# Four block grams of a decayed linear attention as two grams of 96 columns

## The chip, the cores and the metric

One core of one Trainium2 chip. The metric is device time of one execution in microseconds (us). Executions of one kernel scatter here: the 182 executions of the kernel before in the rounds of the experiments took 601.9 to 610.6 us, with a standard deviation of 1.4. In the 20 profiles the start (the time before the stretch defined below) takes 178.0 to 182.3 us, and what follows the stretch 108.7 us in each. PE's clock is half for 10 to 31 us of it, but the start is not simply longer where there is more half clock (178.0 us in e5 and 182.1 in f3, with 10.2 us each), so why it varies is not shown. By the states on record, all timed executions were in the fast state but one, of s2. Two sizes are used: the whole time (a median), and **the stretch**, which leaves that noisy start out: from the 161st of batch one's 216 z records to the first product of batch four (before: from 178.7 to 492.9 us of the span). It is worked out from the starts of the records in the trace and holds all the changed work of the six units but the making of the new masks.

## The reference, cut to what matters

```python
def _attn_ref(r, k, v, w, u):              # (4, 8, 768, 48) each, u (8, 48)
    for t in range(S):
        cur = np.einsum('bhd,bhe->bhde', u[None] * kt, vt)
        y[:, :, t] = np.einsum('bhd,bhde->bhe', rt, state + cur)
        state = wt[:, :, :, None] * state + np.einsum('bhd,bhe->bhde', kt, vt)

def _moe_ref(x, w_tok1, w_tok2, w_ch1, w_ch2):       # x (4, 768, 384) = y, heads side by side
    xt = x.transpose(0, 2, 1)
    h = np.maximum(xt @ w_tok1, 0.0) @ w_tok2
    u = x + h.transpose(0, 2, 1)
    return u + np.maximum(u @ w_ch1, 0.0) @ w_ch2
```

All is float32. A token's r meets an earlier token's k through the product of all w between the two.

## The kernel before

The kernel works on 12 units of 256 tokens (three per batch). Inside 64 tokens it builds the weights r·k in blocks that double: at block size b (2, 4, 8, 16, 32) `gram` multiplies k of the left block of each pair with r of the right one, a masked copy on VectorE (DVE) takes the wanted squares out of PSUM, and `join` then multiplies k and r by the decay over their block, so that the next size can use them. Units 6 to 11, called the near units (`i >= NEAR`), get the diagonal in another way, and are the only ones that the change touches. The token and channel products of the mixer (h_ps, z_ps, q_ps) fill TensorE (PE) between these pieces: the work of a unit is woven between the mixer products of the batch before it.

```python
        def gram(l):
            b = 1 << l
            ...
            right = r_.rearrange("p (n two b) -> p n two b", two=2, b=b)[:, :, 1, :]
            g = L["g"] = ps_g.tile([128, 2, 512], f32, name="gram")
            for ca in range(UC * A):
                fours(lambda q, j, rows, cols: pe.matmul(
                    g[cols, q, ts(ca, 32)], k_[rows, ds(ca * 128 + j * T, T)],
                    right[rows, ts(2 * ca + j, 32 // b), :], start=True, stop=True))
        ...
        def join(l, w, new):
            ...
            dve.tensor_mul(halves, halves, by)                       # k and r at once, 1024 elements
            dve.tensor_mul(new[:ROWS], wv[:, :, 0], wv[:, :, 1])
        ...
        def block(l):
            gram(l)
            join(l, products[l], products[l + 1])
            pick(l)                                                  # the masked copy
        ...
        for l in range(1, LEVELS):
            pieces.append((1.2, lambda l=l: block(l)))
...
        return [(1.0, begin[1]), tokens, one(carry, rest[0]), update, one(before, rest[1]), one(within, rest[2]),
                *loads, *rest[3:], row0, row1, place]
```

The last line weaves two units: `tokens` (transposes of k), `carry` (products kv_ps), `update` (states, on DVE), `before` and `within` (y_ps) belong to unit i, the pieces `rest` are unit i+1's blocks. `fours` issues four products at a time, one for each quarter of PE's array. The pool of gram tiles has two PSUM buffers, which the transposes xT_ps of batches two and three share. `apool` has two buffers of each name.

## Time and profile before

| | before |
|---|---|
| whole time, median of 3 | 604.07 us (602.54 to 604.15) |
| profiled execution | 601.6 us, mean granted clock 0.983 |
| PE, DVE, ACT busy in the whole span | 95%, 60%, 29% |
| the stretch | 314.20 us |
| of it, PE between two records without work (gaps over 0.1 us) | 2.99 us |

The lines of busy time by engine, by stretch and by group are shown in the prediction. To these belongs one view more, since it is the one that changes most: all waits of PE from 200 us to the end, before the change. Columns: engine, what was waited with, what released it: sum in us, how often, the longest.

```profile
PE gram L307 <- issue: 1.0, 2, 0.7
PE y_ps L476 <- DVE state L457: 0.6, 1, 0.6
PE gram L430 <- DVE rk L341: 0.5, 1, 0.5
PE xT_ps L546 <- DVE x L536: 0.3, 1, 0.3
```

In 400 us PE waits 2.4 us, and only 1.4 us of that is for DVE. Whatever the change saves on PE is gained, and whatever it makes PE wait is lost.

### The profile page before, as it was taken

The page shows a single profiled execution, that of the slowest core. Times are in us where ns is not written, and L with a number is a line of the kernel's source. Part 1 is how long each engine was busy: PE and PEld are TensorE (multiplying, and loading weights), DVE is VectorE, ACT ScalarE, POOL GpSimd, SP SyncE. Part 2 cuts the span into 40 slices and gives each one's busy share as a digit, 9 for nine tenths or more (in the row PEclk, how much of TensorE's full clock was granted, in tenths as well). Part 3 has the DMA queues.
Part 4 walks back from the last instruction along what each step waited for, and adds up shares of the span by engine and source line. Part 5 has one row for each costly group of instructions (what it writes and reads, how often), then busy time and mean ns, then how long its engine had stood idle before and what let it go on. Part 6 is the DMA issues. An engine that isn't in the chain of part 4 may idle for free.

```text
span 601.6 us, 18874 instructions
## 1 busy us (share of the span) xinstructions
PE 570.0 (95%) x8596; PEld 486.6 (81%) x8596; DVE 361.0 (60%) x599; ACT 177.1 (29%) x428; POOL 7.2 (1%) x32
## 2 busy tenths in 40 slices
PE   3787899899999989999999999999999999999997
PEld 2776658776888886789989896789898986898987
DVE  5789699999675867666457376528446422040404
ACT  6155444422433313241141231231313312302020
POOL 4000000000000000000000000000000000000000
PEclk9997599999999999999999999999999999999999
DMA  8534564620233235141124103001200000000000
GB/s 340 195 83 152 163 199 151 208 70 28 82 110 109 67 82 158 29 133 28 53 57 132 28 28 106 2 2 43 65 2 28 2 27 0 1 20 8 27 2 27
DMA packets 22976, 45.85 MB, mean 76 GB/s; under 512 B 2512, under 2 KB 14928, under 8 KB 22896
## 3 DMA queue, kind: packets, MB, share of 16 engines
q1 hardware_dynamic: 22752, 44.64, 23.3%
q8 instruction: 67, 1.10, 0.8%
q14 instruction: 13, 0.11, 0.1%
q10 hardware_dynamic: 144, 0.00, 0.0%
HBM read 39.91 MB, written 4.72 MB: 74 GB/s over the span
## 4 chain that ended last, share of the span: by engine, by line
PE 79%; DVE 13%; DMA 3%; issue 3%; ACT 2%; SPq 0%; DVEq 0%; ACTq 0%
PE z_ps L554 29%; PE q_ps L588 24%; PE gram L307 7%; PE h_ps L534 4%; PE h_ps L527 4%; DVE rk L341 3%; DMA x<-in_w_ch_dram 2%; PE h_ps L564 2%; PE kv_ps L440 2%; PE y_ps L489 2%; PE y_ps L476 2%; PE gram L430 2%; DVE at L323 2%; PE xT_ps L546 1%; DVE scratch L218 1%
## 5 line engine op out<-in xcount | busy, mean ns | idle before, releaser
L554 PE MATMUL z_ps<-xT,wch 128*128 128x256 f32 x864 | 195.9, 382 | 1.6 <-ACT z L556 1.6
L554 PEld LDWEIGHTS z_ps<-xT,wch 128*128 128x128 f32 x864 | 161.0, 190 | 23.8 <-ACT z L556 2.8
L556 ACT ACTIVATE z<-z_ps 128x256 f32<-128x256 f32 x144 | 55.0, 382 | 171.3 <-PE z_ps L554 158.2
L588 PE MATMUL q_ps<-wch,z 128*128 128x192 f32 x528 | 94.6, 329 | 0.0
L588 PEld LDWEIGHTS q_ps<-wch,z 128*128 128x128 f32 x528 | 86.1, 190 | 1.4
L588 PE MATMUL q_ps<-scratch,z 128*128 128x192 f32 x396 | 70.0, 328 | 0.0
L307 PE MATMUL gram<-rk 48*64 48x32 f32 x3072 | 62.7, 234 | 6.6 <-issue 3.2
L307 PEld LDWEIGHTS gram<-rk 48*64 48x64 f32 x3072 | 58.2, 152 | 12.4 <-issue 6.4
L341 DVE TENSOR_TENSOR rk<-rk,decay 112x1024 f32<-112x1024 f32 x36 | 44.0, 1223 | 35.7 <-PE gram L307 26.1
L588 PEld LDWEIGHTS q_ps<-scratch,z 128*128 128x128 f32 x396 | 64.4, 190 | 0.4
L341 DVE TENSOR_TENSOR rk<-rk,w 112x1024 f32<-112x1024 f32 x36 | 44.0, 1223 | 28.9 <-PE gram L307 23.9
L580 DVE TENSOR_TENSOR z<-z 128x768 f32<-128x768 f32 x11 | 10.5, 957 | 65.6 <-ACT z L556 65.6
L527 PE MATMUL h_ps<-x,wtok 128*128 128x384 f32 x96 | 35.6, 518 | 0.0
L534 PE MATMUL h_ps<-h,wtok 128*128 128x384 f32 x96 | 35.3, 492 | 0.0
L323 DVE COPY_PREDICATED at<-mask,gram 128x512 f32<-128x512 uint8 x36 | 32.2, 895 | 0.0
L457 DVE TENSOR_TENSOR state<-state,kv_ps 128x192 f32<-128x192 f32 x40 | 14.2, 356 | 24.4 <-PE kv_ps L440 23.5
L331 ACT COPY at<-gram 16x256 f32<-16x256 f32 x48 | 17.4, 363 | 33.7 <-PE gram L307 32.5
L536 DVE TENSOR_TENSOR x<-x,h_ps 128x384 f32<-128x384 f32 x24 | 13.3, 553 | 23.1 <-PE h_ps L534 23.1
L527 PEld LDWEIGHTS h_ps<-x,wtok 128*128 128x128 f32 x96 | 18.5, 201 | 10.4 <-issue 0.6
L534 PEld LDWEIGHTS h_ps<-h,wtok 128*128 128x128 f32 x96 | 16.4, 190 | 9.6 <-ACT h L529 2.6
L431 ACT COPY kT<-gram 128x512 f32<-128x512 f32 x24 | 14.0, 585 | 28.5 <-PE gram L430 28.3
L318 ACT COPY at<-gram 32x256 f32<-32x256 f32 x48 | 17.4, 363 | 14.2 <-PE gram L301 13.7
(84 smaller groups left out, 514.9 us busy)
## 6 DMA issues: line engine op xcount, KB each, us to landing
rk<-in_rkw_dram SPq DMA_DIRECT2D x36, 192.0 KB, 3.4
x<-in_w_ch_dram SPq DMA_DIRECT2D x10, 512.0 KB, 4.3
vt<-in_v_dram SPq DMA_DIRECT2D x12, 384.0 KB, 4.4
out_dram<-o SPq DMA_DIRECT2D x24, 192.0 KB, 1.9
rp<-in_near_dram SPq DMA_DIRECT2D x12, 384.0 KB, 3.6
scratch<-in_w_ch_dram SPq DMA_DIRECT2D x8, 512.0 KB, 4.3
w<-in_rkw_dram SPq DMA_DIRECT2D x18, 192.0 KB, 3.2
rk<-in_rkw_dram SPq DMA_DIRECT2D x6, 512.0 KB, 6.5
```

What stands on the lines that cost most here:

```text
L307: fours(lambda q, j, rows, cols: pe.matmul(g[cols, q, ts(ca, 32)], k_[rows, ds(ca * 128 + j * T, T)], right[rows, ts(2 * ca + j, 32 // b), ...
L318: act.copy(at[p:p + b, :, ts(c, A), b:], g[ds(p + c * b, b)])
L323: dve.copy_predicated(out=dst, data=g.rearrange("p q (m b) -> p q m b", b=b), mask=masks[l].rearrange("p x t -> p (x t)").rearrange("p (m ...
L331: act.copy(at[p:p + b, :, :, n * 2 * b + b:(n + 1) * 2 * b], g[p:p + b, :, :, ts(n, b)])
L341: dve.tensor_mul(halves, halves, by)
L431: act.copy(L["kT"][:, c], ps)
L457: dve.tensor_add(new, new, got)
L527: pe.matmul(sums[i], wtok1[:, c, ts(i, 128)], xs[bt][:, c, :], start=(c == 0), stop=(c == C - 1))
L534: pe.matmul(ps, wtok2[:, i, ts(c, 128)], h1[:, i, :], start=(i == 0), stop=(i == DTOK // 128 - 1))
L554: pe.matmul(ps, wch1[:, m, ts(jt, 128)], xT[:, m, ts(s, SEG)], start=(m == 0), stop=(m == DM // 128 - 1))
L556: act.activation(zs[s][:, jt, :], ps, AF.Relu)
L588: pe.matmul(ps, a[:, j, :], b[:, j, :], start=(j == 0), stop=(j == HJ - 1))
```

## The change

Block sizes 2 and 4, and sizes 8 and 16, get one gram each. Of four neighbouring blocks (0 to 3) of size b, the pairs of both sizes are (0→1), (0,1→2,3) and (2→3). The moving side holds six groups of columns: r of blocks 1, 2, 3 as they are, and r of blocks 2 and 3 decayed over the one or two blocks between. So 96 columns take the place of two times 32, four grams become two, and k and r are joined over four blocks at once.

```diff
+        def two_blocks(l):
+            b = 1 << l
+            ...
+                t = apool.tile([128, COLS], f32, name="rp")
+                ...
+                act.copy(y[:, :, 0:4:3], of[:, :, 1:3])
+                act.copy(y[:, :, 5], of[:, :, 3])
+                dve.tensor_mul(y[:, :, 1:5:3], of[:, :, 2:4], by[:, :, 1:3]...)
+                dve.tensor_mul(y[:, :, 2], y[:, :, 4], by[:, :, 1]...)
+            for c in range(UC):
+                g = ps_g.tile([128, 2, 512], f32, name="gram")
+                ...
+                    fours(lambda q, j, rows, cols: pe.matmul(
+                        g[cols, q, ts(a, 96)], k_[rows, ds((c * A + a) * 128 + j * T, T)],
+                        rw[c][rows, ts(2 * a + j, 96)], start=True, stop=True))
+            ... (two small products of w, then k by w of three blocks, r from the moving side, new decay)
+            for c in range(UC):
+                ...
+                for q, first in enumerate((0, 3, 5)):
+                    n = (3 - q) * b
+                    dve.copy_predicated(out=to[:, :, :, (q + 1) * b:], data=got[:, :, :, first * b:first * b + n], ...)
 ...
+        if i >= NEAR:
+            return pieces + [(1.8, lambda l=l: two_blocks(l)) for l in (1, 3)] + [(0.9, lambda: block(5))]
         for l in range(1, LEVELS):
             pieces.append((1.2, lambda l=l: block(l)))
 ...  (masks for four blocks, made once; the near rows' loads come one step later, for they share the tiles "rp")
+        if i + 1 >= NEAR:
+            rest[2] = (rest[2][0], lambda f=rest[2][1]: (load_near(i + 1), f()))
```

More of the change, by code (lines that the diff above doesn't have):

```diff
@@ L259, in begin @@
             if i >= NEAR:
+                products[3], products[5] = w_[:, :COLS // 8], decay[:, :COLS // 32]
                 join(0, products[0], products[1])
@@ L353, in block @@
             pick(l)
+        def two_blocks(l):
+            b = 1 << l
+            w = products[l].rearrange("p (g q) -> p g q", q=4)[:ROWS]
+            k = k_.rearrange("p (g q b) -> p g q b", q=4, b=b)[:ROWS]
+            r = r_.rearrange("p (g q b) -> p g q b", q=4, b=b)[:ROWS]
+            G = COLS // (4 * b) // UC
+            rw, gs = [], []
+            for c in range(UC):
+                t = apool.tile([128, COLS], f32, name="rp")
+                rw.append(t)
+                y = t[:, :COLS // UC * 3 // 2].rearrange("p (g s b) -> p g s b", s=6, b=b)[:ROWS]
+                of, by = r[:, ts(c, G)], w[:, ts(c, G)]
+                act.copy(y[:, :, 0:4:3], of[:, :, 1:3])
+                act.copy(y[:, :, 5], of[:, :, 3])
+                dve.tensor_mul(y[:, :, 1:5:3], of[:, :, 2:4], by[:, :, 1:3].unsqueeze(3).to_broadcast([ROWS, G, 2, b]))
+                dve.tensor_mul(y[:, :, 2], y[:, :, 4], by[:, :, 1].unsqueeze(2).to_broadcast([ROWS, G, b]))
+            for c in range(UC):
+                g = ps_g.tile([128, 2, 512], f32, name="gram")
+                gs.append(g)
+                for a in range(A):
+                    fours(lambda q, j, rows, cols: pe.matmul(
+                        g[cols, q, ts(a, 96)], k_[rows, ds((c * A + a) * 128 + j * T, T)],
+                        rw[c][rows, ts(2 * a + j, 96)], start=True, stop=True))
+            dve.tensor_mul(w[:, :, 2], w[:, :, 2], w[:, :, 3])
+            dve.tensor_mul(w[:, :, 1], w[:, :, 1], w[:, :, 2])
+            dve.tensor_mul(k[:, :, :3], k[:, :, :3], w[:, :, 1:].unsqueeze(3).to_broadcast([ROWS, UC * G, 3, b]))
+            for c in range(UC):
+                y = rw[c][:, :COLS // UC * 3 // 2].rearrange("p (g s b) -> p g (s b)", s=6, b=b)[:ROWS, :, :3 * b]
+                dve.tensor_mul(r[:, ts(c, G), 1:].rearrange("p g q b -> p g (q b)"), y,
+                               w[:, ts(c, G), 0].unsqueeze(2).to_broadcast([ROWS, G, 3 * b]))
+            dve.tensor_mul(products[l + 2][:ROWS], w[:, :, 0], w[:, :, 1])
+            for c in range(UC):
+                to = at_c[:, :, c].rearrange("p q a (m n) -> p q (a m) n", n=4 * b)
+                got = gs[c][:, :, :A * 96].rearrange("p q (m n) -> p q m n", n=6 * b)
+                for q, first in enumerate((0, 3, 5)):
+                    n = (3 - q) * b
+                    dve.copy_predicated(out=to[:, :, :, (q + 1) * b:], data=got[:, :, :, first * b:first * b + n],
+                                        mask=masks4[l][:, q].unsqueeze(1).unsqueeze(3).to_broadcast([128, 2, A * 16 // b, n]))
@@ L361, in load_near @@
     def load_near(i):
-        if i >= NU:
-            return
         L = near_by[i] = [apool.tile([128, COLS], f32, name="kp", bufs=1)]
@@ L401, in nearest, with quarters, masks @@
         return [(0.3, lambda c=c: late(newest(dve), dve, lambda: row(c))) for c in range(UC)] + [
-            (0.2, lambda: (place(), load_near(i + 1)))]
+            (0.2, place)]
     near_by = {}
+    masks4 = {l: const.tile([128, 3, A * 16 >> l], u8, name=f"mask4_{l}") for l in (1, 3)}
     def begin_near():
+        def quarters(l, m):
+            b = 1 << l
+            n = 16 // b
+            pool.memset(m, 1.0)
+            for q in range(3):
+                for base, by in ((-q * b, 1), (q * b + b - 1, -1)):
+                    pool.affine_select(out=m[:, q], in_=m[:, q], compare_op=ALU.is_ge, fill=0.0, base=base,
+                                       pattern=[[-by * 4 * b, 2 * n]], channel_multiplier=by)
+            for j in range(2):
+                dve.tensor_copy(masks4[l][ts(j, T)].rearrange("p q (a n) -> p q a n", a=A),
+                                m[ts(j, T), :, ts(j, n)].unsqueeze(2).to_broadcast([T, 3, A, n]))
+        def masks():
+            t = apool.tile([128, COLS], f32, name="rp")
+            for l in masks4:
+                quarters(l, t[:, ts(l // 2, 48)].rearrange("p (q n) -> p q n", q=3)[:, :, :32 >> l])
         def parities():
@@ L410, in parities @@
             dve.tensor_scalar(odd, odd, -1.0, 1.0, op0=ALU.mult, op1=ALU.add)
-        late(newest(dve), dve, parities)
+        late(newest(dve), dve, lambda: (parities(), masks()))
         late(newest(sp), sp, lambda: sp.dma_start(u_rows, u_all))
-        load_near(NEAR)
     def post(i):
```

## The prediction

> **What bounds the kernel now.** I read the page first (busy time of each engine), then busy time in three stretches, then the timeline of PE, then the groups of instructions of DVE.
>
> ```profile
> PE 570.0 (95%) x8596; PEld 486.6 (81%) x8596; DVE 361.0 (60%) x599; ACT 177.1 (29%) x428; POOL 7.2 (1%) x32
> ```
>
> The view of busy time by stretch cuts the span where the changed code begins: the six near units, 6 to 11, lie between 213 and some 490 us. Its columns are the stretch, its length, each engine's busy time with the count of instructions, the granted PE clock, and DMA.
>
> ```profile
> 0.00:213.00 213.00, 186.66 (x3832) 152.39 (x3832) 172.51 (x263) 85.99 (x199) 6.88 (x29) 0.95 0.44 140
> 213.00:520.00 307.00, 305.02 (x4348) 260.59 (x4342) 167.24 (x298) 78.71 (x197) 0.33 (x3) 1.00 0.16 48
> 520.00:601.60 81.60, 78.33 (x426) 73.57 (x424) 21.21 (x39) 12.36 (x33) 0.00 (x0) 1.00 0.04 15
> ```
>
> In the stretch concerned PE is busy 305.0 of 307 us at full clock, and DVE 167.2, or 54%. The longest waits of PE there sum to about 2 us, near 216 to 225 us, where DVE is still the busier. So time that PE doesn't spend on grams comes off the span one for one, as long as DVE, which gets the added work, doesn't make PE wait. DMA (16% here) and ACT (26%) bound nothing.
>
> What a gram costs is seen in the timeline of PE, from one burst's start to the next one's (columns: start, length, then the group):
>
> ```profile
> 184.32 1.13 PE L284 MATMUL gram<-rp,kp 48*64 48x64 f32 x64
> 185.37 2.43 PE L554 MATMUL z_ps<-xT,wch 128*128 128x256 f32 x10
> ...
> 193.16 1.15 PE L489 MATMUL y_ps<-vt,at 64*64 64x48 f32 x64
> 194.13 1.10 PE L307 MATMUL gram<-rk 48*64 48x32 f32 x64
> 195.16 1.99 PE L554 MATMUL z_ps<-xT,wch 128*128 128x256 f32 x8
> 197.08 1.14 PE L307 MATMUL gram<-rk 48*64 48x32 f32 x64
> 198.15 1.99 PE L554 MATMUL z_ps<-xT,wch 128*128 128x256 f32 x8
> ```
>
> 64 records (each float32 product is two) of 32 columns take 1.03 to 1.07 us, of 48 columns 0.97 (no full-array product follows, so no change of tiling), of 64 columns 1.05. **The count of columns makes no difference from 32 to 64.** By the records' starts in the trace, four records (one per quarter of the array) start some 7 ns apart, then comes a gap, and the period of four is 58 ns in all three. So the narrow grams waste half their slots: that is what the change is after.
>
> [...]
> - [...] The trace: 1223 (L341), 554 (L383), 951 to 957 (L382, L580). I size the new DVE operations with it.
> - [...] The trace: from the last record of a gram to the next full product 150 ns instead of about 15, and about 90 ns more on the way in.
>
> **The change, part by part** (per near unit, of which there are six).
>
> PE before: four grams L307 (blocks 2, 4, 8, 16). Each is 16 groups of four records: 16 x 58 = 0.93 us. Four are 3.71 us. After: two grams of 64 records with 96 columns[...]: 1.36 us each, 2.72 together. Saved 0.99 us.
> Tilings: the order of instructions shows that the fourth gram and the last one (block 32, L301) stood alone among full products before, and that now every gram follows kv, y or the weighted values, which are already in quarters. Two stays in the tiled mode fewer, at about 0.15 + 0.09 us each less some 0.05 for the new junction: 0.4 us. Sum 1.4 us a unit, **8.5 us for six**. This is on the path, since PE is full.
>
> DVE, from these rows (the groups of the stretch from 213 to 520 us; columns: count, busy, mean ns, idle before):
>
> ```profile
> L341 DVE TENSOR_TENSOR rk<-rk,decay 112x1024 f32<-112x1024 f32 x18 | 22.0, 1223 | 26.1 <-PE gram L307 19.0 <-PE gram L301 7.0
> L341 DVE TENSOR_TENSOR rk<-rk,w 112x1024 f32<-112x1024 f32 x16 | 19.6, 1223 | 24.3 <-PE gram L307 20.0 <-DMA rk<-in_rkw_dram 4.3
> L323 DVE COPY_PREDICATED at<-mask,gram 128x512 f32<-128x512 uint8 x18 | 16.1, 894 | 0.0
> ```
>
> Removed: four joins of r and k with 1024 elements (4.9 us), four small products (0.9), three masked copies (2.7; by record the one with runs of two elements takes 1.29 and the others 0.70): 8.5 us, and on ACT the four copies L331 (4 x 0.363 = 1.5).
> Added per pair of blocks: r on the moving side 2 x (0.42 + 0.29) us for 256 and 128 elements; w products 0.57 (0.38 for the second pair), and 0.28 (0.19) for the new decay; k 0.96 for 768 elements; r 2 x 0.56 for 384; masked copies with 384, 256 and 128 elements for each of two chunks, 2.5 to 2.8. That is 7.2 us for the first pair and 6.6 for the second: 13.8 us. Net **+5.3 us of DVE a unit, +32 us in all**: DVE goes from 54 to about 64% of that stretch. On ACT +2.6 - 1.5 us of copies a unit. POOL and DVE make new masks once (some 14 and 4 small instructions, started early). None of this is on the path by itself. The round trips PE to DVE and back fall from five to three a unit.
>
> **Rivals.**
> 1. *The gain is pure PE time, and DVE stays hidden.* For: DVE idles 46% of the stretch, the woven order leaves about 12 us between a unit's two new grams. Then 604.1 - 8.5 = 595.5 us.
> 2. *DVE bursts hold up PE.* Each new gram is followed by some 5 to 7 us of DVE work in a row, and both buffers of the gram's PSUM pool are now taken at once instead of one. Where a burst falls beside products that DVE has to drain (q_ps, x + h_ps), or beside transposes that take the same two buffers, PE waits. By the order of instructions that is so in unit 7 and unit 10 (xT transposes of the second and third batch come two products after the gram: I estimate 1.2 us each), unit 6 (DVE still behind, the second gram needs about 7 us of DVE after the first: 1 us more than now), unit 8 (its output sum lies behind the copies: 1 us), unit 11 (the 3.8 us of L580 to L583 come behind the burst: 1 us). In all about 5 us, badly known: 2 to 10. Then 600 to 601; at 10, 605.
> 3. *The 96-column gram is slower than 85 ns per four*[...]. With two at a time, 160 ns: 2.6 us each, 5.1 against 3.71, and the change would lose 1.0 us a unit. [...] Unlikely.
> 4. *The loads stay the bound at 96 columns* (58 ns): 1.86 instead of 2.72, a gain of 13.7 us. [...]
> 5. *A transfer becomes late*: near data now comes one step later, for its tiles are used by the new code. It took 3.6 us to land, and the rows that need it come two steps later, so it should be hidden.
>
> **Range and chances.** 604.1 - 8.5 + 5 = 600.5; rounded down to 600, as the author's order may hide more of the bursts than I count. The whole saving with no wait gives 595.5, the waits at 10 us give 605.5; 594 to 606 should hold it 8 times in 10. Faster by over 2% means under 592[...]: 0.05. Slower by over 2% means 20 us of waits, four times my count: 0.03. Within 2%: 0.92.
>
> **What would show each step.** Right: gram bursts of 96 columns 1.35 to 1.55 us from start to the next start; no gram alone among full products; PE busy in the stretch down by about 8 us; DVE about 32 us up; new waits of PE on gram buffers, q_ps sums and x + h_ps of 2 to 10 us. Wrong: bursts of 0.95 or of 2.6 us (step PE); waits of PE over 12 us or a DVE that is the chain's larger part after 213 us (rival 2 undersized); a wait on near or rk transfers (rival 5).

What the trace of before shows for its estimates: the z products of 256 columns come every 215 to 217 ns, 0.84 ns a column. If grams keep that pace, 96 columns take 81 ns per four records, an estimate; the 85 ns of the prediction (1.36 us a gram) are the author's estimate too. Against rival 3, at the same pace 64 columns, two quarters at a time, would need 108 ns (and 96 columns about the 160 of the prediction), and the trace has 58. For rival 4 speaks that four records take 58 ns where 64 columns are loaded (L307) and 33 where 32 are (L301), with 32 columns on the moving side of both; against it, the 81 ns. The added DVE operations are sized by those of the same length: 1024 elements took 1223 ns, 768 took 951 to 957, 384 took 554, 256 about 420 and 128 about 290.

## The result, and the profile after

| | before | after |
|---|---|---|
| whole time, median of 6 and 6 executions | 604.15 us (602.54 to 605.33) | 605.47 us (604.27 to 606.78) |
| ratio | | 1.0021, 95% interval 1.0001 to 1.0042 |
| profiled execution | 601.6 us, clock 0.983 | 603.9 us, clock 0.985 |
| the stretch | 314.20 us | 316.26 us |

A ratio is the mean time of one kernel's fast executions over that of the other's in the same rounds, so not quite the ratio of the medians quoted. The result is right. It lies inside the range, and within 2%, but with the other sign: instead of 4 us less, 1.3 us more. By the record an execution of the change lasts 2.1 us longer than its span in the profile, one of the kernel before 1.7, so 0.3 of the 1.3 us lie outside of all that the profiles show.

The lines after that answer to those of before. First the busy time of the page, then the stretch from 213 to 520 us (length, busy time of PE, its weight loads, DVE, ACT, POOL with counts, granted clock, DMA share, GB/s), then the timeline of PE at a gram that ran at full clock, with the product behind it:

```profile
PE 565.7 (94%) x7828; PEld 481.9 (80%) x7828; DVE 384.7 (64%) x729; ACT 182.4 (30%) x452; POOL 9.5 (2%) x46
...
213.00:520.00 307.00, 299.07 (x3650) 253.74 (x3641) 188.39 (x417) 82.42 (x215) 0.33 (x3) 0.99 0.17 51
...
288.77 1.52 PE L379 MATMUL gram<-rp,rk 48*64 48x96 f32 x64
290.22 2.22 PE L649 MATMUL q_ps<-wch,z 128*128 128x192 f32 x12
```

PE did what was hoped: 299.07 us busy instead of 305.02 in the same window, and a gram of 96 columns takes 1.45 us from its start to the next product's. By the starts of the records, four of them begin within 20 ns, and the period of four is 83 ns. DVE has 21 us more in this window. But the window now leaves PE idle for 7.9 us instead of 2.0, and the clock is 0.99 instead of 1.00. The longest waits of PE from 200 us on (two of 0.3 and 0.2 us are left out):

```profile
PE gram L379 <- DVE rp L374: 2.0, 1, 2.0
PE xT_ps L607 <- DVE at L395: 2.0, 2, 1.3
PE z_ps L615 <- ACT z L617: 1.2, 2, 0.6
PE q_ps L649 <- DVE o L663: 1.2, 2, 0.7
PE z_ps L615 <- DVE o L687: 0.8, 1, 0.8
PE gram L491 <- DVE rk L342: 0.5, 1, 0.5
```

They are of four kinds. **Unit 6** comes first: its second gram waits for its moving side (the timeline of PE, with the wait in brackets):

```profile
216.56 1.15 PE L537 MATMUL y_ps<-state,rk 48*64 48x48 f32 x64
219.75 2.56 PE L379 MATMUL gram<-rp,rk 48*64 48x96 f32 x64 [2.04 <-DVE rp L374]
222.24 4.21 PE L649 MATMUL q_ps<-wch,z 128*128 128x192 f32 x12
```

The gram behind the wait takes 2.56 us instead of 1.52, and twelve q products 4.21 us instead of the 2.22 seen above. The granted clock is half from 220.4 to 227.3 us, as the view of that window shows (columns as above, the clock third from the end; 0.51 because the last 0.15 us of the window lie behind the half clock):

```profile
220.60:227.40 6.80, 6.77 (x92) 6.02 (x89) 5.23 (x16) 0.00 (x0) 0.00 (x0) 0.51 0.59 176
```

In the trace of before no half clock is granted between 75 us and the end.

**The transposes xT** come second. Here is DVE in batch two, behind a gram that ended at 244.9 us, and then PE:

```profile
245.06 0.72 DVE L395 COPY_PREDICATED at<-mask,gram 128x384 f32<-128x384 uint8 x1
...
246.72 0.97 DVE L384 TENSOR_TENSOR rk<-rk,decay 112x768 f32<-112x768 f32 x1
247.62 0.72 DVE L395 COPY_PREDICATED at<-mask,gram 128x384 f32<-128x384 uint8 x1
248.20 0.53 DVE L597 TENSOR_TENSOR x<-x,h_ps 128x384 f32<-128x384 f32 x1
```

```profile
247.06 0.52 PE L607 MATMUL xT_ps<-ident,x 128*128 128x128 f32 x3 [0.69 <-DVE at L395]
```

The transposes take the gram's PSUM buffers, so they wait for the masked copies of the first chunk, the last of which ends 2 us behind the gram. The sums x + h (L597) stand in the same queue behind such copies.

**The z drains on ACT** are third. ACT now also copies r to the moving side, and does so in order (ACT, then PE):

```profile
262.58 0.38 ACT L617 ACTIVATE z<-z_ps 128x256 f32<-128x256 f32 x1 [0.91 <-PE z_ps L615]
264.81 0.42 ACT L371 COPY rp<-rk 112x256 f32<-112x256 f32 x1 [1.85 <-DMA rp<-in_near_dram]
...
265.35 0.65 ACT L617 ACTIVATE z<-z_ps 128x256 f32<-128x256 f32 x2
```

```profile
265.77 1.56 PE L615 MATMUL z_ps<-xT,wch 128*128 128x256 f32 x6 [0.64 <-ACT z L617]
```

The copy wants a tile "rp", which the near rows hold until they have landed and been summed; ACT stops for it, and two z drains that were ready stand behind. Rival 5 of the prediction, a near transfer that comes late, happens here, only not where it was looked for. **The q and output sums on DVE** (L663, L687), behind bursts of masked copies, are fourth, 0.4 to 0.9 us each.

The sum of all this, worked out from the record starts of the two profiled executions over the stretch. A record counts from its start to the next one's, less any gap over 0.1 us, and the gaps are counted apart:

| us in the stretch | before | after | difference |
|---|---|---|---|
| grams of blocks 2 to 32 | 34.81 | 27.49 | -7.32 |
| q products | 99.26 | 101.30 | +2.04 |
| y_ps from the weights (L489, now L550) | 7.85 | 8.89 | +1.04 |
| all other products | 169.29 | 169.83 | +0.54 |
| gaps of PE over 0.1 us | 2.99 | 8.75 | +5.76 |
| sum | 314.20 | 316.26 | +2.06 |

### The profile page after: what moved, and what is told of

It is laid out like the page before. It is cut to its first block, busy times and chain, and to the rows that moved or that the text cites. A ratio compares the mean times of both kernels' runs of the same rounds, so it can differ in the third digit from the quotient of the medians.

```text
span 603.9 us, 17514 instructions
## 1 busy us (share of the span) xinstructions
PE 565.7 (94%) x7828; PEld 481.9 (80%) x7828; DVE 384.7 (64%) x729; ACT 182.4 (30%) x452; POOL 9.5 (2%) x46
## 4 chain that ended last, share of the span: by engine, by line
PE 72%; DVE 17%; issue 4%; DMA 3%; ACT 3%; SPq 0%; DVEq 0%; ACTq 0%
PE z_ps L615 24%; PE q_ps L649 21%; PE h_ps L588 5%; PE gram L308 4%; PE h_ps L595 3%; PE kv_ps L501 2%; PE y_ps L550 2%; DVE at L395 2%; PE gram L491 2%; PE y_ps L537 2%; PE h_ps L625 2%; DVE rk L342 2%; PE gram L379 1%; DMA rp<-in_near_dram 1%; DVE state L518 1%
## 5 line engine op out<-in xcount | busy, mean ns | idle before, releaser
L649 PE MATMUL q_ps<-wch,z 128*128 128x192 f32 x528 | 96.2, 333 | 0.2 <-DVE z L675 0.2
L649 PEld LDWEIGHTS q_ps<-wch,z 128*128 128x128 f32 x528 | 88.3, 193 | 2.2 <-DVE z L675 0.5
L641 DVE TENSOR_TENSOR z<-z 128x768 f32<-128x768 f32 x11 | 10.5, 957 | 68.9 <-ACT z L617 68.9
L395 DVE COPY_PREDICATED at<-mask,gram 128x384 f32<-128x384 uint8 (+2 forms) x72 | 33.9, 477 | 19.0 <-PE gram L379 18.4
L308 PEld LDWEIGHTS gram<-rk 48*64 48x64 f32 x1536 | 33.3, 170 | 8.3 <-issue 3.6
L308 PE MATMUL gram<-rk 48*64 48x32 f32 x1536 | 35.6, 250 | 4.6 <-issue 2.2
L342 DVE TENSOR_TENSOR rk<-rk,decay 112x1024 f32<-112x1024 f32 x24 | 29.4, 1223 | 12.7 <-PE gram L302 6.8
L342 DVE TENSOR_TENSOR rk<-rk,w 112x1024 f32<-112x1024 f32 x24 | 29.3, 1224 | 6.2 <-PE gram L308 3.3
L597 DVE TENSOR_TENSOR x<-x,h_ps 128x384 f32<-128x384 f32 x24 | 13.2, 549 | 19.5 <-PE h_ps L595 19.4
L371 ACT COPY rp<-rk 112x256 f32<-112x256 f32 x24 | 10.1, 420 | 49.3 <-issue 19.8
L379 PE MATMUL gram<-rp,rk 48*64 48x96 f32 x768 | 19.7, 250 | 2.1 <-DVE rp L374 2.0
L491 PE MATMUL gram<-ident,rk 128*128 128x128 f32 x96 | 17.9, 314 | 3.6 <-ACT kT L492 2.9
```

What stands on the lines that cost most here:

```text
L308: fours(lambda q, j, rows, cols: pe.matmul(g[cols, q, ts(ca, 32)], k_[rows, ds(ca * 128 + j * T, T)], right[rows, ts(2 * ca + j, 32 // b), ...
L379: fours(lambda q, j, rows, cols: pe.matmul(g[cols, q, ts(a, 96)], k_[rows, ds((c * A + a) * 128 + j * T, T)], rw[c][rows, ts(2 * a + j, 96 ...
L395: dve.copy_predicated(out=to[:, :, :, (q + 1) * b:], data=got[:, :, :, first * b:first * b + n], mask=masks4[l][:, q].unsqueeze(1).unsquee ...
L491: pe.transpose(ps[:, a, :], k_[:, ts(c * A + a, 128)], ident)
L597: dve.tensor_add(x[:, c, :], x[:, c, :], ps)
L649: pe.matmul(ps, a[:, j, :], b[:, j, :], start=(j == 0), stop=(j == HJ - 1))
```

## The experiments

Eighteen kernels ran. The theories, in the order in which they came up: the copies and products added on DVE are simply too much for it; the PSUM buffers held by two gram tiles stop the transposes; the copies on ACT block the z drains; unit 6 alone costs it all; the place of the DVE work behind a gram matters and not its amount; and last, PE's idleness brings down its own clock. The expectations are quoted as they were recorded, and a letter in them stands for a theory of that moment. This table is read together with them: whole time as ratio to before in the same rounds, then for the profiled execution the stretch, the gaps of PE over 0.1 us in it, and the time at half clock in it.

| run | whole, ratio (95%) | stretch | gaps | half clock |
|---|---|---|---|---|
| before | 1 | 314.20 | 2.99 | 0 |
| the change | 1.0021 (1.0001 to 1.0042) | 316.26 | 8.75 | 6.8 |
| e1_no_masked_copies (wrong result) | 0.9970 (0.9951 to 0.9989) | 312.57 | 8.78 | 0 |
| e2_copies_from_sbuf (wrong result) | 1.0126 (1.0088 to 1.0164) | 320.55 | 13.78 | 3.4 |
| e3_unit6_as_before | 1.0020 (1.0007 to 1.0034) | 314.57 | 8.33 | 0 |
| e4_before_with_vector_work | 1.0010 (0.9987 to 1.0033) | 314.30 | 2.74 | 0 |
| e5_only_2_with_4 | 0.9982 (0.9964 to 1.0000) | 311.69 | 4.31 | 0 |
| e6_only_8_with_16 | 0.9942 (0.9915 to 0.9969) | 310.68 | 3.38 | 0 |
| e7_half_the_columns (wrong result) | 0.9877 (0.9827 to 0.9927) | 305.73 | 6.52 | 0 |
| e8_near_rows_on_gpsimd | 1.0243 (1.0203 to 1.0284) | 327.81 | 18.60 | 10.2 |
| f1_moving_copies_on_gpsimd | 1.0027 (1.0009 to 1.0044) | 315.79 | 8.30 | 6.8 |
| f3_both_on_gpsimd | 1.0187 (1.0139 to 1.0235) | 326.72 | 17.16 | 10.2 |
| g2_transposes_elsewhere | 1.0050 (1.0031 to 1.0069) | 315.88 | 10.12 | 3.4 |
| g5_three_causes_mended | 1.0023 (1.0006 to 1.0039) | 315.11 | 8.92 | 0 |
| r1_one_step_later | 0.9981 (0.9962 to 1.0000) | 312.54 | 8.33 | 0 |
| r2_burst_first | 1.0191 (1.0159 to 1.0222) | 326.41 | 9.89 | 13.7 |
| r3_burst_third | 1.0014 (0.9994 to 1.0034) | 314.68 | 3.22 | 0 |
| r4_mixed | 0.9908 (0.9880 to 0.9936) | 309.62 | 2.61 | 0 |
| s1_wait_filled | 1.0042 (1.0025 to 1.0058) | 314.88 | 8.73 | 0 |
| s2_wait_half_filled | 1.0010 (0.9993 to 1.0027) | 313.01 | 7.67 | 0 |

The three wrong results are wrong on purpose: only the time was asked for.

### Is the saving on PE real? Half the columns, and each pair alone

**e7_half_the_columns**: the paired grams multiply 48 of the 96 columns.

```diff
-                        g[cols, q, ts(a, 96)], k_[rows, ...], rw[c][rows, ts(2 * a + j, 96)], ...
+                        g[cols, q, ts(a, 48)], k_[rows, ...], rw[c][rows, ts(2 * a + j, 96)]
+                          .rearrange("p (g s) -> p g s", s=6 * b)[:, :, :3 * b], ...
```

> The changed kernel with 48 instead of 96 columns of the moving side per product, the masked copies reading the same number of elements from a narrower gram (wrong result on purpose). It measures what the columns cost by themselves. By the prediction's working, four records then take 58 ns instead of 83: ten grams of batches two and three fall from 14.5 us to 10.3 to 10.7 us together. Whether the whole falls by as much tells whether TensorE still sets the pace there: if so batches two and three take about 260.5 us; if the waits take the gain (they are set by other engines), about 262 to 264 us.

The paired grams of batches two and three fell from 8.71 to 6.31 us and from 5.82 to 4.20, that is 1.45 to 1.05 us each: at 48 columns the gram costs what one of 32 or 64 columns costs in the kernel before, and at 96 it costs 0.40 us more. Batches two and three together took 258.3 us, less than the 260.5 expected. The stretch fell by 10.5 us, the whole to 596.95 us. Of these 10.5, 4.8 are the columns of twelve grams at full clock, 2.2 fewer gaps, and most of the rest is the half clock that did not come. So what PE is spared does shorten the stretch.

**e5_only_2_with_4** pairs the first two sizes alone, **e6_only_8_with_16** the last two alone; the other two sizes stay single grams of 32 columns.

```diff
 e5:
-            return pieces + [(1.8, lambda l=l: two_blocks(l)) for l in (1, 3)] + [(0.9, lambda: block(5))]
+            return pieces + [(1.8, lambda: two_blocks(1))] + [(1.2, lambda l=l: block(l)) for l in (3, 4, 5)]
 e6:
+            return pieces + [(1.2, lambda l=l: block(l)) for l in (1, 2)] + [(1.8, lambda: two_blocks(3)), (0.9, lambda: block(5))]
 ...  (both: which decay goes to which block size; e6 also loads the near rows one piece later)
```

> Only blocks 2 and 4 from one gram; 8, 16 and 32 as before. Half of the gain in grams: a pair saves 2 x 0.93 - 1.36 = 0.5 us a unit, 3 us in six. If the waits come with each pair, from both gram buffers held and moving copies that wait for tiles, about half of them stay: from the start of the third batch's work to the last batch (314.2 us before, 316.3 changed) 314 to 316 us, whole 604 to 605. If one pair alone carries the loss, this run or the next is near 312 us and the other near 316.

> Only blocks 8 and 16 from one gram, which also leaves one gram fewer alone among full products; near rows loaded one piece later than in the changed kernel, so that the tiles don't deadlock. Saves about 0.5 + 0.2 us a unit. If the waits follow the number of pairs: 313.5 to 315.5 us on the same stretch, whole 603.5 to 605.

Either pair alone gains: 2.5 and 3.5 us of the stretch, and 603.40 (the interval of its ratio reaches 1.0000) and 600.37 us against 604.45 in the same rounds. The grams cost 4.6 and 4.2 us less, the gaps rise by only 1.3 and 0.4. Both pairs together save 7.3 us at the grams, and the gaps rise by 5.8. **The loss is not the sum of the parts**: it comes when both stand in one unit. One caution on e6: its near rows come one piece later, and no run tells what that alone does to its gaps; e5, whose gaps rise little too, has no such change.

### Is it DVE's load?

**e1_no_masked_copies** leaves out the masked copies of the paired grams (33.9 us of DVE, mean 477 ns); the order on PE stays the same.

```diff
-                    dve.copy_predicated(out=to[:, :, :, (q + 1) * b:], data=got[...], mask=masks4[l]...)
+                    pass
```

> The changed kernel without its masked copies of the paired grams (wrong result on purpose; the buffers of the grams are then never read and come free when their products end). This takes some 34 us of VectorE time out, 5.6 us a unit, and leaves TensorE's instructions as they are. Theory A (the bursts of VectorE, and the gram buffers that they hold, make TensorE wait and eat a gain of some 8 us): 597 to 600 us, ratio to the kernel before 0.989 to 0.994; TensorE's waits on VectorE in batches two and three go from about 5.5 us to under 2. Rival B (the grams of 96 columns are themselves dearer than the four narrow ones, or the new order of TensorE costs it): 604 to 606 us, as the changed kernel.

**e4_before_with_vector_work** gives the kernel before four more DVE operations in each near unit (24 of 1.22 us, in place on w, without effect), so that DVE has the load of the changed kernel or more.

```diff
             join(l, products[l], products[l + 1])
+            if i >= NEAR and l in (1, 3):
+                for n in range(2):
+                    dve.tensor_tensor(out=w_[:ROWS], in0=w_[:ROWS], in1=w_[:ROWS], op=ALU.max)
```

> The kernel before with two more VectorE operations of 1024 elements in place (the larger of w and w, so nothing changes in value) behind the first and the third join of each of the six near units: 12 x 2 x 1.22 = 29 us of VectorE work, as much as the change adds net; TensorE and the buffers as before. If VectorE's load alone makes TensorE wait (A1): 607 to 612 us. If load matters little where the gram buffers are not both held (A2): 604 to 606 us.

The busy time in the window from 213 to 520 us, first of e1 (columns as above), then of e4:

```profile
213.00:520.00 307.00, 299.07 (x3681) 254.39 (x3678) 161.68 (x346) 83.25 (x217) 0.33 (x3) 1.00 0.18 52
```

```profile
213.00:520.00 307.00, 305.18 (x4365) 260.41 (x4358) 189.31 (x318) 78.63 (x196) 0.34 (x3) 1.00 0.16 48
```

With DVE at 161.7 us, less than in the kernel before, PE is busy 299.07 us and its gaps are 8.78 us, as in the changed kernel. With DVE at 189.3 us, PE has no more gaps than before. So the load of DVE as such is no cause. (The whole of e1, 602.52 us, lies between the two ranges expected.) One caution on e4: the added operations hung on w alone, so the build spread them over DVE's queue, between other work, and did not keep them right behind the join. e1's stretch is 3.7 us shorter with the half clock absent, not with fewer gaps.

### Is it the place? The same burst behind the first and behind the third join

**r2_burst_first** and **r3_burst_third** give the kernel before two operations of 1.22 us on k and r, which must follow the join, in one place each.

```diff
             join(l, products[l], products[l + 1])
+            if i >= NEAR and l == 1:        # r3: l == 3
+                for x in (k_, r_):
+                    dve.tensor_tensor(out=x[:ROWS], in0=x[:ROWS], in1=x[:ROWS], op=ALU.max)
```

> The kernel before, with two more 1024-element operations of DVE (in place, 2 x 1.22 us, result unchanged) right behind the first join of each near unit, which they must follow; PE's work untouched. If DVE work at that place holds up PE's drains: stretch from 314.2 to 317-321 us (0.5 to 1.2 us a unit), whole 607 to 611. Rival, that DVE work alone is hidden at 60% load: 314.2 within 0.5, whole 604 to 605.

> The same two operations behind the third join of each near unit, the place of the second pair. If the place decides: less lost than with the first join, 314.2 to 316 us, whole 604 to 606. If a chain that is 2.4 us longer costs the same anywhere: as the run with the first join.

The waits of PE in r2:

```profile
PE xT_ps L549 <- DVE x L539: 4.9, 2, 2.6
PE y_ps L479 <- DVE state L460: 2.5, 1, 2.5
PE z_ps L557 <- DVE z L623: 1.4, 1, 1.4
```

14.6 us of DVE work behind the first joins cost 12.2 us of the stretch, 6.9 of it in gaps (the rest goes with 13.7 us at half clock); the same work behind the third joins costs 0.5. That is more than was expected of the first place, and what was expected of the third. PE waits for the sums x + h, for the state and for a sum of z, none of which has to do with grams: they stand behind the burst in DVE's queue, as its timeline in r2 shows:

```profile
247.46 2.39 DVE L355 TENSOR_TENSOR rk<-rk 112x1024 f32<-112x1024 f32 x2
249.77 1.01 DVE L539 TENSOR_TENSOR x<-x,h_ps 128x384 f32<-128x384 f32 x2
```

**r1_one_step_later** takes the changed kernel and hands out both pairs one step later.

```diff
+        if i + 1 >= NEAR:
+            return [(1.0, begin[1]), tokens, carry, update, one(before, rest[0]), one(within, rest[1]),
+                    *loads, rest[2], row0, row1, place]
```

> The changed kernel, with each near unit's two paired grams handed out one step later among the products. Stretch from unit 6's state products to the end of batch three (before 314.2 us, changed 316.3). If the lost time comes from where the DVE burst of the first pair falls (behind the state products, ahead of the x + h sums and the q and z drains), the waits of PE move or vanish: second h products back from 9.1-9.5 to 8.3-8.7 us a batch, z of batch two back from 50.8 to about 48.5, stretch 311 to 313, whole 600 to 602. Rival, that the first pair's DVE and ACT operations cost it wherever they stand: stretch 316 to 317, whole 605 to 606. Third outcome: the burst hits other drains (q or y) there, the waits move by kind and their sum stays.

The longest waits of PE in r1:

```profile
PE z_ps L615 <- DVE o L687: 1.9, 1, 1.9
PE q_ps L649 <- ACT z L617: 1.8, 1, 1.8
PE q_ps L649 <- DVE o L663: 1.1, 1, 1.1
```

The stretch is 3.7 us shorter than the change's, as the theory of the place wanted, and the whole 602.79 us a little above its range. But its reason is another: the gaps are 8.33 instead of 8.75 us. The waits for xT and for unit 6 have become waits for sums of the output and for a z drain, so the third outcome named in the expectation is what came, and the gain goes with the absent half clock. Moving the bursts moves the waits.

### Mending single waits

**g2_transposes_elsewhere**: the transposes of batches two and three get PSUM buffers of another pool.

```diff
-            if bt in (0, B - 1):
+            if True:
```

> The changed kernel with the transposes of x in batches two and three in the other PSUM pool (the one of kv and y), as in batches one and four, so that they no longer rotate through the two gram buffers. Theory A2 (both gram buffers held through the masked copies stop the transposes, and the h products behind them): h products and transposes of batches two and three from 9.1 + 9.5 + 2.1 + 2.1 to 8.5 + 8.3 + 2.1 + 2.1 us, those two batches 1.5 us shorter (263 us), whole 603 to 604.5. Rival: the transposes now wait for kv and y instead, no change or worse.

The waits for xT (2.3 us) vanish, and these are new (waits of PE in g2):

```profile
PE h_ps L595 <- DVE x L597: 1.8, 1, 1.8
PE z_ps L615 <- DVE x L597: 1.1, 1, 1.1
```

So the PSUM buffers were where the wait was seen, and freeing them gained nothing: the sums x + h behind the same burst held PE next. The whole, 607.00 us, is no better than the change's, as the rival expected, though not for kv and y.

**e2_copies_from_sbuf** lets the masked copies read a constant in SBUF in place of the gram, so that no copy holds a gram's buffer.

```diff
-                got = gs[c][:, :, :A * 96].rearrange("p q (m n) -> p q m n", n=6 * b)
+                got = wch1[:, :2, :A * 96].rearrange("p q (m n) -> p q m n", n=6 * b)
```

> The changed kernel with the masked copies kept in number and size, but read from a weight matrix in SBUF instead of the gram's PSUM buffer (wrong result on purpose). VectorE keeps its load, about 384 us; the gram buffers come free when their products end, and the copies wait for no product. If it is VectorE's load that delays TensorE (A1): 603 to 606 us, as the changed kernel. If it is that both buffers of the pool are held through the burst (A2): 600 to 603 us, with the waits of the xT transposes on the masked copies (2.0 us) gone and little else changed.

Inconclusive: the copies no longer follow the grams, and the order on all engines changed with them. PE waited 3.6 us for the kT copies on ACT, and the gaps rose to 13.8 us. It only agrees with g2 in that free buffers did not help.

**f1_moving_copies_on_gpsimd** takes the copies to the moving side off ACT.

```diff
-                act.copy(y[:, :, 0:4:3], of[:, :, 1:3])
-                act.copy(y[:, :, 5], of[:, :, 3])
+                pool.tensor_copy(y[:, :, 0:4:3], of[:, :, 1:3])
+                pool.tensor_copy(y[:, :, 5], of[:, :, 3])
```

> The changed kernel with the plain copies of r into the moving side's tile moved from ScalarE to GpSimd, which is idle. In the changed kernel's profile these copies stood at the head of ScalarE's queue waiting for a tile that the near rows still held (19.8 + 14.9 + 7.3 us of idle ScalarE before them), and the drains of z behind them came late: z products took 2.6 us more in batch two. Theory D (ScalarE's queue is blocked at its head by copies that wait for one of two shared tiles): z in batch two back from 50.8 to 49.3 us or less, batches two and three together from 264.6 to 262.5 to 263.5 us, whole 602 to 604. Rival (z is late for VectorE's drains of the last products, not for ScalarE's): z stays at 50 to 51 and the two batches at 264.5 us.

The two waits for z drains at 265.8 and 272.4 us are gone, and the z products of batch two fall from 50.83 to 49.40 us. That shows the block on ACT to be real. But gaps sum to 8.30 us again: unit 6's wait is 2.13 us (a copy takes 560 ns on GpSimd instead of 420 on ACT), and the z products wait 1.4 us for the output sums L687 instead of 0.8. So the theory's numbers were missed: 264.0 us for the two batches and 606.08 for the whole. The expectation also reads too much into ACT's idle time: of its three figures only the 7.3 us are put down to the near rows' sums, 14.9 to the gram, and 19.8 to nothing that the profile shows.

**e3_unit6_as_before** leaves unit 6 with its four single grams.

```diff
-        if i >= NEAR:
+        if i > NEAR:
             return pieces + [(1.8, lambda l=l: two_blocks(l)) for l in (1, 3)] + ...
```

> The changed kernel with unit 6, the first of the third batch, left on the four narrow grams. In the profile of the changed kernel TensorE waited 2.0 us before unit 6's second gram, and the granted clock then fell to half for 6.8 us. Theory C (the change as such is worth something, and unit 6, where VectorE is still behind with the work of the first batch, gives it back with the clock that falls after the long wait): no half clock after 211 us, and 601 to 603.5 us, ratio 0.995 to 0.999. Rival (units 7 to 11 lose as much as they gain anyway, and the half clock comes in any case): 604 to 606 us.

The wait of 2.04 us and the half clock go, and with them unit 6's saving, 1.9 us by the same sum (3.2 us of half clock and 0.4 of gaps less, yet the stretch is only 1.7 us under the change's). The whole, 605.83 us, is not better. Five units still have gaps 5.3 us over those of before.

**g5_three_causes_mended** has all three: unit 6 as before, transposes elsewhere, and the moving copies on DVE.

```diff
-            return pieces + [(1.8, ...) for l in (1, 3)] ...     (from `i >= NEAR` to `i > NEAR`)
-                act.copy(y[:, :, 0:4:3], of[:, :, 1:3])  ...      (both copies to dve.tensor_copy)
-            if bt in (0, B - 1):                                  (to `if True:`)
```

> Three edits together: unit 6 as before (no long wait there), the transposes of x in the other PSUM pool, and the plain copies for the moving side on VectorE instead of ScalarE (so that they stand in line behind the sums that free their tiles and block no drain of z; +1.1 us of VectorE a pair). If the three causes found (clock and wait at unit 6, gram buffers, ScalarE's queue) are the loss: five units' gain of 6 us less 2 us of drains behind VectorE's bursts: 310 us on the stretch from the third batch's work to the last batch, whole 599.5 to 601.5, faster than both kernels. If VectorE's load counts instead: 314 to 316 us.

8.92 us of gaps. With these three mended, other waits of the same sum stand in their place (1.8 us for x + h, 1.7 us for a sum of q). The stretch, 315.11 us, lies in the range given to DVE's load, and DVE had the two copies more; but e1 and e4 speak against load as such.

**e8_near_rows_on_gpsimd** and **f3_both_on_gpsimd** put the near rows' two products on GpSimd, f3 the moving copies as well.

```diff
-            dve.tensor_mul(rr, rr, k.unsqueeze(1).to_broadcast([128, 2, DM]))
-            dve.tensor_mul(rr[:, 0], rr[:, 0], u_rows)
+            pool.tensor_mul(rr, rr, k.unsqueeze(1).to_broadcast([128, 2, DM]))
+            pool.tensor_mul(rr[:, 0], rr[:, 0], u_rows)
```

> The changed kernel with the two products of the near rows (0.95 + 0.55 us, twice a unit, 18 us in all) moved from VectorE to GpSimd. If VectorE's load is the cause after all (A1), the drains of q come earlier: q in batches two and three back from 42.8 and 43.1 to about 42.1 us each, the two batches together 262.5 to 263.5 us. By the run of the kernel before with 29 us more of VectorE work (its two batches 264.6 against 264.2 us) load as such hardly counts: then 264 to 265.5 us, or more, as the tiles of the near rows are held longer by a slower engine and the copies for the moving side wait for them (D).

> Both moves at once: moving copies and near-row products on GpSimd. D alone: as the first move alone, 262.5 to 263.5 us for batches two and three. If both causes count: 261 to 262.5 us, whole 600.5 to 603 us. If GpSimd is too slow and holds the tiles: over 264 us.

Both are slower, e8 by 2.4% and f3 by 1.9%, with 276.1 us for batches two and three in each: a product of 768 elements takes 2034 ns on GpSimd and 951 on DVE, one of 384 takes 1351 and 554. The chain of the near rows got longer, the "rp" tiles stayed taken for longer, and the gaps went to 18.6 and 17.2 us. DVE had less to do, and PE waited more.

### Is it PE's own clock?

Over all runs of this study, the traces have 31 waits of PE of 1.0 to 1.9 us in the stretch, and none of them is followed by half clock. Of the 16 of 2.03 to 3.20 us, 12 are, for 3.4 or 6.8 us, which begin 2.0 to 4.3 us after the wait did. The change has exactly one wait of that kind. **s1_wait_filled** puts 64 records of idle products into it (the real gram overwrites what they write), **s2_wait_half_filled** 32.

```diff
-                for a in range(A):
+                for x, a in [(x, a) for x in [k_] * (2 * (i == NEAR and l == 3 and c == 0)) + [rw[c]] for a in range(A)]:
                     fours(lambda q, j, rows, cols: pe.matmul(
                         g[cols, q, ts(a, 96)], k_[rows, ds((c * A + a) * 128 + j * T, T)],
-                        rw[c][rows, ts(2 * a + j, 96)], start=True, stop=True))
+                        x[rows, ts(2 * a + j, 96)], start=True, stop=True))
```

> The changed kernel, with 64 records of idle products put into PE's 2.04 us wait of unit 6 (k against itself, into the gram's own buffer, overwritten by the real gram; the result stays right). Nothing gets shorter; PE only does 1.4 us more. If the half clock after that wait comes from PE's idleness and costs about 3.4 us: no half clock between 200 and 500 us, the gram and 12 q products after it at full speed, the stretch from unit 6's state products to the end of batch three down from 316.3 to 312.5-313.5 us, whole 601.5 to 603.5. Rival, that those products are slow for another reason (DVE's burst or DMA beside them): they stay slow, stretch 316 to 317.5, whole 605 to 607.

> The same with 32 records: some 1.3 us of the wait stay. In all runs so far no wait under 1.9 us was followed by half clock, and 12 of 16 waits of over 2 us were. If that holds: no half clock, stretch 312.5 to 313.5 us, whole 601.5 to 603.5, as with 64 records. If any stop of PE there brings it: half clock stays, stretch 316 to 317.

The timeline of PE in s2:

```profile
216.72 1.15 PE L537 MATMUL y_ps<-state,rk 48*64 48x48 f32 x64
218.10 0.89 PE L379 MATMUL gram<-rk 48*64 48x96 f32 x32 [0.23 <-DVE at L395]
219.92 1.89 PE L379 MATMUL gram<-rp,rk 48*64 48x96 f32 x64 [0.93 <-DVE rp L374]
221.74 2.22 PE L649 MATMUL q_ps<-wch,z 128*128 128x192 f32 x12
```

The gram starts 3.20 us after the y products, as in the changed kernel (3.19), but the half clock is gone and the twelve q products take 2.22 us again. In s1 it is gone too. The stretch is 313.01 us in s2 (as expected) and 314.88 in s1 (expected 312.5 to 313.5; it shows two gaps of 0.65 and 0.86 us more among q products, the first put down to nothing that the profile shows, the second to DVE's sum L675). The five profiles in which unit 6's second gram waits 2.03 to 2.13 us unfilled (the change, e8, f1, f3, g2) all show the half clock behind it. So in the profiled executions **PE's idleness brings the half clock, and work without use keeps it away** (five of five there with the wait unfilled, none of two with it filled). Its cost in the profiled execution, by the rows of the sum above (s2 without its idle products against the change): q 2.07, grams 0.77, y 0.37, together 3.2 us.

The whole times did not follow: 606.31 us in s1 (20 executions) and 604.56 in s2 (19 fast ones of 20), where 601.5 to 603.5 was expected. That is a miss, and s2's gain on the change (ratios 1.0010 and 1.0021) is inside the noise. Each kernel has one profile, but the record has the mean granted clock of every execution. It is 0.983 and 0.984 on average in s1 and s2, and 0.983 in the kernel before of the same rounds: more half clock in the executions that were not profiled is not what kept the two slow, and what did stays open. Over the six executions of the change it is 0.979, over the 182 of the kernel before 0.982. The difference of 0.003 is 1.8 us of 604, an estimate with a standard error of 1.3. So the half clock is shown for the profiled execution; what it is worth in the median stays open, between 0 and 3 us.

### The version that follows

**r4_mixed** pairs 2 with 4 in unit 6 alone, and 8 with 16 in units 7 to 11 alone, each where it had cost least.

```diff
+        if i == NEAR:
+            return pieces + [(1.8, lambda: two_blocks(1))] + [(1.2, lambda l=l: block(l)) for l in (3, 4, 5)]
+        if i > NEAR:
+            return pieces + [(1.2, lambda l=l: block(l)) for l in (1, 2)] + [(1.8, lambda: two_blocks(3)), (0.9, lambda: block(5))]
```

> Pair 2 with 4 in unit 6 alone, pair 8 with 16 in units 7 to 11 alone: each part where the earlier runs saw it gain. If the parts add up: stretch about 47.2 + 133.5 + 127.9 = 308.6 us (8 with 16 everywhere: 310.7), whole 598 to 599.5. If unit 6's gain came from something the other pair's presence changes: 310 to 311, whole 600 to 601.

All waits of PE from 200 us on in r4:

```profile
PE q_ps L653 <- DVE o L667: 1.2, 1, 1.2
PE gram L310 <- DVE rk L386: 0.4, 1, 0.4
```

The stretch is 309.62 us (1 us more than the sum of the parts), the gaps 2.61, under those of before. The whole is 599.67 us against 604.05 in the same rounds, 0.9% less: a right result, just above its range, and faster than both kernels. (As in e6, the near rows come one piece later.) Against e6 (0.9942, with an interval that overlaps) it is not told apart by times.

## Why the prediction was right or wrong, point by point

- **PE is the bound, and what it saves counts one for one**: right in kind. e7 took away nothing but columns, 4.8 us of PE at full clock, and the stretch fell by that and more, for gaps (2.2 us) and half clock went too.
- **The gram of 96 columns takes 1.36 us, 1.35 to 1.55 by record**: right, 1.45 us; 83 ns per four records, where the author's estimate was 85. Rivals 3 and 4 (2.6 and 0.95 us) are out.
- **8.5 us saved in six units**: right in kind, too high. At full clock (the table's differences less what the half clock cost) the grams cost 8.1 us less, but the y products from the weights 0.7 more (1.08 us each instead of 0.97, for six of them now stand before the gram of block 32, which starts 148 ns after their last record, where a gram of 32 columns started after 38) and other products 0.5 more: 6.9 us.
- **DVE +32 us, hidden by itself**: right that its amount is hidden (e1 and e4). The durations were right one by one (the masked copies of a pair took 2.9 us, where 2.5 to 2.8 was reckoned), and their sum over the whole span grew by 35 us, from 391.1 to 426.2. Yet DVE's busy time grew by 24 us only, from 361.0 to 384.7. Records of DVE overlap where one follows another, as the copy at 247.62 us shown above, 0.72 us long, and the sum that starts at 248.20; a sum of durations counts that twice.
- **"In all about 5 us, badly known: 2 to 10", for new waits of PE**: this is the step that failed. Its idle part was sized well: 5.8 us measured. But each wait was counted at its length alone. The entry for unit 6, "the second gram needs about 7 us of DVE after the first: 1 us more than now", became a wait of 2.04 us and 6.8 us at half clock behind it, worth 3.2 us more in the profiled execution. The waits term is then 5.8 + 3.2 = 9.0 us, and -6.9 + 9.0 is the +2.1 of the stretch. The prediction took the full clock of the kernel before for granted. This account holds for the profiled execution; for the medians, s1 and s2 did not confirm the 3.2 us.
- **Which waits they would be**: partly right. Unit 6, the transposes of units 7 and 10 (0.69 and 1.33 us where 1.2 each was estimated) and output sums were named. The copies on ACT that stop for a shared tile were not, and rival 5 was put aside with "so it should be hidden": f1 shows it was not, through ACT.
- **The sign**: -4 us predicted, +1.3 measured in the medians, +2.1 in the stretch. The range held by half a us, and only because its upper end allowed for 10 us of waits.
- **Readings of the profile before**: right.

Two things stay open. One is why both pairs in one unit cost 4 us more gaps than the two alone: r1, g2, g5 and f1 show that mending or moving one wait puts another in its place, so the slack between the grams of a unit is used up as a whole, but no run measures that slack, so this is argued and not shown. The other is how often the half clock comes in executions that were not profiled, and what else kept s1 and s2 slow there.

## What to carry to other kernels

When an engine is 99% busy, a change that shortens its work and lengthens a neighbour's burst is judged by what stands in the neighbour's queue behind that burst, not by the neighbour's load: 14.6 us of DVE work cost 12.2 us behind one join, 0.5 behind another, and 29 us cost 0.1 of the stretch where it could float. Try the parts of such a change one by one, since each alone may gain where the whole loses. And count a long wait of PE at its length plus what a halved clock behind it may cost: here 12 of the 16 waits of 2.03 to 3.20 us were followed by half clock and none of the 31 of 1.0 to 1.9 us, and behind one wait of 2.04 us it cost 3.2 us in the profiled execution.

## More figures from the traces

- The first full product behind a gram starts 150 ns after the gram's last record with 32 columns (before, L307) and 172 ns with 96 (the change, L379). Products in quarters (before, L476) start 17 ns after it, and grams start 28 to 39 ns behind products in quarters (before, L307 behind L476, L489 and L440).
- Masked copies from PSUM on DVE: in the change (L395) 128, 256 and 384 elements took 358, 424 and 650 ns on average (650 is the mean of some at 570 to 580 and some at 720). In the kernel before (L323) one of 512 elements took 0.70 us, but 1.29 us where it goes in runs of two elements.
